# A Fourier mixing layer with its two products taken in the other order, beside attention in one kernel

## The chip, the cores and the metric

The kernel runs on one core of one Trainium2 chip. The metric is device time in microseconds of one execution. All inputs and outputs are float32 in the chip's memory (DRAM). The engines are TensorE (PE; its weight load is PEld), VectorE (DVE), ScalarE (ACT), GpSimd (POOL) and SyncE (SP), which issues every transfer of this kernel.

## The reference

Two layers on separate inputs of 2048 rows and 1024 channels, put side by side into one output of 2048 x 2048.

```python
def _A_ref(x, wqkv, wo):                 # attention, H = 32 heads of Dh = 32
    qkv = (x @ wqkv).reshape(B, S, 3, H, Dh).transpose(2, 0, 3, 1, 4)
    q, k, v = qkv[0], qkv[1], qkv[2]
    p = softmax(einsum("bhqd,bhkd->bhqk", q, k) * Dh ** -0.5)
    o = einsum("bhqk,bhkd->bhqd", p, v)
    return o.transpose(0, 2, 1, 3).reshape(B, S, D) @ wo

def _B_ref(x, dft_seq_re, dft_seq_im, dft_hid_re, dft_hid_im):   # Fourier mixing
    a = einsum("bsd,ed->bse", x, dft_hid_re)
    b = einsum("bsd,ed->bse", x, dft_hid_im)
    return einsum("ts,bse->bte", dft_seq_re, a) - einsum("ts,bse->bte", dft_seq_im, b)

return concatenate([_A_ref(...), _B_ref(...)], axis=-1)
```

With C for the cosine matrix over the sequence, N for the sine one, and R, I for the channel ones, the Fourier half is y = C (x R') - N (x I').

## The kernel before

**Dense products.** Every dense product (qkv, the two of the Fourier half, the output projection) is done in blocks of 128 x 512 with one step of Winograd's form of Strassen: a product of 2 x 2 halves takes 7 half-size products (numbered 1 to 7 in the code; `ORDER` is the order in which they are taken) and additions before and behind. Each operand tile is split into a rounded high part (a cast) and a residual (raw minus high), both in the fast float32 format, and each product of two tiles is three matmuls: high by high, low by high, high by low. So a block of depth 512 (4 chunks) is a **group** of 12 matmuls and one of depth 1024 a group of 24, all accumulating in one PSUM bank. `group` (L421) records them. `piece` makes a stationary operand of 4 chunks (tiles h and l), `moving` a moving one (a slot of two halves, twelve slots in a ring). Both call `fetch`, which loads one tile (raw), loads others (g) and adds or subtracts them on GpSimd or VectorE (L507), and `halves` (L528 cast, L531 residual).

**The Fourier half.** `dense1` takes x by both channel matrices: stationary x, 8 tiles, moving the 16 tiles of R and I; 7 x 8 x 2 groups of 12. It stores a = x R' and b = x I' as ab_d. `dense2` then does C a (m = 0) and N b (m = 1), 7 x 8 groups of 24 each; C and N are the stationary operands (in_ct), a and b the moving ones. The result of m = 0 goes to y_d, and behind m = 1 it is loaded again and the imaginary half subtracted from it (L1029). `gather` reads each finished group out of PSUM: it adds it to a running sum, kept in SBUF (slots 16 to 19, L984, L986) or in memory (class `Far`, x_d, L998, L1000), or to the sum that gives a result (L1024); what lies in memory is loaded into a tile c (L971), four of which go round.

**Attention.** Per head: scores of 128 x 1024 (L1322, two matmuls each), their row maxima on VectorE (L1328, negm), exponentials on ScalarE for the row sums (L1331); then transposed scores (L1447), exponentials of them (L1456) into tiles pt, and 64 small matmul records at a time with V (L1479).

**What sets the order.** All operations are recorded with their dependencies and given out by a planner (`Plan`, and the loop at the end) that keeps a clock per engine from fixed costs (a wide matmul 0.2274, a copy out of PSUM 0.685, a subtraction on GpSimd 1.31) and writes the order of every engine by hand. On TensorE the attention streams S, T and V alternate with the dense matmuls, which are called **fills** and come strictly in the order in which the dense functions record them: qkv, dense1, dense2, projection. A fill is given when its share of all fills is no further on than attention's share. Each engine then runs its own list in order and waits on semaphores where a producer is late.

Of the kernel before, what the change touches and what calls it, by code (L numbers as in the profile page):

```python
# [16 lines left out]
P = 128  # L17
# [208 lines left out]
def kernel(  # L226
# [25 lines left out]
    ab_d = [[[dram.tile([P, NB], F32, name=f"ab_d{m}_{e}_{k}") for k in range(NS)] for e in range(2)] for m in range(2)]  # L252
    s1_d = [dram.tile([P, 4, P], F32, name=f"s1_d{i}") for i in range(8)]
    t1_d = [dram.tile([P, NB], F32, name=f"t1_d{n}") for n in range(8)]
# [5 lines left out]
    u3_d = [[dram.tile([P, NB], F32, name=f"u3_d{i}_{m}") for m in range(2)] for i in range(8)]  # L260
    s2_d = [[dram.tile([P, 4, P], F32, name=f"s2_d{i}_{k}") for k in range(4)] for i in range(8)]
    t2_d = [[dram.tile([P, NB], F32, name=f"t2_d{m}_{k}") for k in range(8)] for m in range(2)]
    x_d = [[{w: dram.tile([P, NB], F32, name=f"x_d{i}_{m}_{w}") for w in (1, 6, 5)} for m in range(2)] for i in range(4)]
    u4_d = [[dram.tile([P, NB], F32, name=f"u4_d{m}_{i}") for i in range(8)] for m in range(2)]
    y_d = [[dram.tile([P, NB], F32, name=f"y_d{i}_{e}") for e in range(2)] for i in range(NS)]
# [119 lines left out]
    FILL = 3 * (7 * 24 * 4 + 7 * 16 * 4 + 7 * 8 * 16 + 2 * 8 * 4)  # L385
# [15 lines left out]
    banks = []  # L401
    fills = []
# [8 lines left out]
    def group(terms, n, finish):  # L411

        box = {}
        n *= 3
        k = 0
        for a, b in terms:
            for (u, v), after in (((0, 0), (a[0].made[0], b[0].made[0])), ((1, 0), (a[0].made[1],)), ((0, 1), (b[0].made[1],))):
                def emit(a=a, b=b, u=u, v=v, k=k):
                    if k == 0:
                        box["ps"] = bank()  # L420
                    nc.tensor.matmul(box["ps"], a[1]((a[0].hi, a[0].lo)[u]()), b[1]((b[0].hi, b[0].lo)[v]()), start=k == 0, stop=k == n - 1)  # L421

                o = op("PE", MM, emit, after, [a[0].users, b[0].users] if v else [])
                fills.append((o, k == 0, n - k))
                k += 1
        frees.append(finish(lambda: box["ps"], o))

    def groups(parts):
# [4 lines left out]
        for c in range(depth):  # L433
            for j, (u, v) in enumerate(((0, 0), (1, 0), (0, 1))):
                for i, (terms, _) in enumerate(parts):
# [10 lines left out]
                    fills.append((last[i], first, 3 * (depth - c) - j))  # L446
# [514 lines left out]
    def gather(what, X, Y, u3, to, wrote, part=None):  # L961
# [18 lines left out]
        def finish(ps, last):  # L980
# [25 lines left out]
            def put(at, ausers, alast, kind, to, wrote, part):  # L1006
# [15 lines left out]
                def emit():  # L1022
                    box["y"] = pre.tile([P, NB], F32, name="e", tag="e", bufs=NE)
                    nc.vector.tensor_tensor(out=box["y"], in0=at(), in1=ps(), op=kind)  # L1024
# [6 lines left out]
                wrote.append(op("SP", ISSUE, lambda: nc.sync.dma_start(to, box["y"]), [done], [users], rank, 256))  # L1031
# [27 lines left out]
    ab_st = [[[[] for _ in range(NS)] for _ in range(2)] for _ in range(2)]  # L1059

    def dense1():
        s1 = [[] for _ in range(8)]
        s2 = [[] for _ in range(8)]
        t1 = [[] for _ in range(8)]
        u3 = [[[], []] for _ in range(8)]

        def a_terms(p, i):
            q = lambda r, k: xb[8 * r + i, :, 4 * k : 4 * k + 4, :]
            return {
                1: [(1, q(0, 0), [])], 2: [(1, q(0, 1), [])], 4: [(1, q(1, 1), [])],  # L1070
                5: [(1, q(1, 0), []), (1, q(1, 1), [])],
                6: [(1, q(1, 0), []), (1, q(1, 1), []), (-1, q(0, 0), [])],
                7: [(1, q(0, 0), []), (-1, q(1, 0), [])],
                3: [(1, q(0, 1), []), (-1, s1_d[i], s1[i])],
            }[p]

        def b_terms(p, n):
            m, c = divmod(n, 4)
            q = lambda k, e: wd[m, 4 * k + c, :, e * NB : e * NB + NB]
            return {  # L1080
                1: [(1, q(0, 0), [])], 2: [(1, q(1, 0), [])], 3: [(1, q(1, 1), [])],
                5: [(1, q(0, 1), []), (-1, q(0, 0), [])],
                6: [(1, q(1, 1), []), (-1, q(0, 1), []), (1, q(0, 0), [])],
                7: [(1, q(1, 1), []), (-1, q(0, 1), [])],
                4: [(1, t1_d[n], t1[n]), (-1, q(1, 0), [])],
            }[p]

        def load_b(x, n):
            p = ORDER[x]
            B[x][n] = moving((8 * x + n) % 12, b_terms(p, n), (t1_d[n], t1[n]) if p == 6 else None)  # L1090

        B = [[None] * 8 for _ in ORDER]
        for n in range(4):
            load_b(0, n)
        X = {}
        for x, p in enumerate(ORDER):
            for i in range(8):
                a = piece(a_terms(p, i), (s1_d[i], s1[i]) if p == 6 else None)
                if i == 0:
                    for n in range(4, 8):  # L1100
                        load_b(x, n)
                if p == 1:
                    X[i] = accs(SUMS[i]) if i < 4 else [Far(x_d[i - 4][m]) for m in range(2)]
                for m in range(2):
                    h = DONE.get(p)
                    to = ab_d[m][h[1]][8 * h[0] + i] if h else None
                    group(
                        ((chunk(a, c), (B[x][4 * m + c], whole)) for c in range(4)), 4,
                        gather(p, X[i][m], None, (u3_d[i][m], u3[i][m]), to, ab_st[m][h[1]][8 * h[0] + i] if h else None),
                    )  # L1110
                if i % 2:
                    load_b(x + 1, i // 2) if x < 6 else load_ab(0, i // 2)

    AB = {}
    t2 = [[[] for _ in range(8)] for _ in range(2)]

    def load_ab(step, k):
        m, x = divmod(step, 7)
        p = ORDER[x]

        q = lambda r, e: (ab_d[m][1 - e][8 * r + k], ab_st[m][1 - e][8 * r + k])
        terms = {
# [4 lines left out]
            4: [(1, t2_d[m][k], t2[m][k]), (-1, *q(1, 0))],  # L1127
        }[p]
        AB[step, k] = moving((8 * (7 + step) + k) % 12, terms, (t2_d[m][k], t2[m][k]) if p == 6 else None)

    def dense2():

        y_st = [[[], []] for _ in range(NS)]
        u4 = [[[] for _ in range(8)] for _ in range(2)]
        for m in range(2):
            s2 = [[[], []] for _ in range(8)]

            def a_terms(p, i, k0):
                q = lambda r, k: ct[8 * r + i, :, 16 * m + 8 * k + k0 : 16 * m + 8 * k + k0 + 4, :]
                return {  # L1140
                    1: [(1, q(0, 0), [])], 2: [(1, q(0, 1), [])], 4: [(1, q(1, 1), [])],
                    5: [(1, q(1, 0), []), (1, q(1, 1), [])],
                    6: [(1, q(1, 0), []), (1, q(1, 1), []), (-1, q(0, 0), [])],
                    7: [(1, q(0, 0), []), (-1, q(1, 0), [])],
                    3: [(1, q(0, 1), []), (-1, s2_d[i][2 * m + k0 // 4], s2[i][k0 // 4])],
                }[p]

            X = {}
            for x, p in enumerate(ORDER):
                step = 7 * m + x  # L1150
                for i in range(8):
                    if p == 1 and i % 2 == 0:
                        X[i // 2] = accs(SUMS[i // 2])

                    def terms():
                        for k in range(0, 8, 4):
                            if i == 0 and k:
                                for c in range(4, 8):
                                    load_ab(step, c)
                            a = piece(a_terms(p, i, k), (s2_d[i][2 * m + k // 4], s2[i][k // 4]) if p == 6 else None)  # L1160
                            for c in range(4):
                                yield chunk(a, c), (AB[step, k + c], whole)

                    h = DONE.get(p)
                    t, e = (8 * h[0] + i, 1 - h[1]) if h else (0, 0)
                    to = out[t * P : t * P + P, D + e * NB : D + e * NB + NB] if m else y_d[t][e]
                    group(
                        terms(), 8,
                        gather(p, X[i // 2][i % 2], None, (u4_d[m][i], u4[m][i]), to,
                               [] if m else y_st[t][e], (y_d[t][e], y_st[t][e]) if m and h else None),  # L1170
                    )
                    if step < 13 and i % 2:
                        load_ab(step + 1, i // 2)
# [376 lines left out]
    done = 0.0  # L1550
# [5 lines left out]
    while nf < len(fills) or any(place[n] < len(s) for n, s in streams.items()):  # L1556
# [56 lines left out]
        if nf < len(fills):  # L1613
            o, first, left = fills[nf]
# [7 lines left out]
        if fill is not None and (not ok or (not first and left <= HB) or nf / (FILL - RES) <= done / ATT):  # L1622
            pl.start(fill)
            nf += 1
# [55 lines left out]
```

## Time and profile before

| | |
|---|---|
| runs | 2941.31, 2941.32, 2941.8 us; median 2941.32 |
| profiled execution, its span | 2940.6 us |
| granted TensorE clock | 1.000 |
| TensorE busy | 2931.5 us, 14922 matmul records |
| VectorE, ScalarE, GpSimd busy | 2275.1, 2271.7, 956.6 us |
| dense1: first store of a running sum (x_d), last store of a result (ab_d) | 842.6, 1472.8 us |
| dense2: first and last load of a second operand from ab_d, last load of y_d | 1305.0, 2700.3, 2777.2 us |
| end of the last attention matmul, of the last matmul | 2747.8, 2936.8 us |

A row of the groups gives line, engine, operation, output and inputs, count, then busy time, the mean of one in ns, and the idle time ahead of them with what ended it. A row of the windows gives a stretch, its length, and per engine the busy time and count (PE, PEld, DVE, ACT, POOL), the granted clock, the share of the transfer engines and GB/s. A row of the chain or the timeline gives a start and a length in us. "128x512" is partitions by elements.

### The profile page before, as it was taken

How to read it: one execution, taken by the hardware profiler on the slowest of the kernel's cores; microseconds unless marked ns; L12 is line 12 of the kernel's file. 1: busy time of each engine (PE TensorE's matmuls, PEld its weight loads, DVE VectorE, ACT ScalarE, POOL GpSimd, SP SyncE). 2: the span in 40 equal slices, each digit the busy share in tenths (PEclk: the TensorE clock that was granted, in tenths of full speed). 3: DMA queues.
4: the chain of work that ended last, by engine and by line, in shares of the span. 5: the costliest groups of instructions: out<-in, count | busy, mean ns of one | idle time of the engine just before them, and what ended most of it. 6: DMA issues, size and time to landing. Idle time of an engine off the chain costs nothing.

```text
span 2940.6 us, 45778 instructions
## 1 busy us (share of the span) xinstructions
PE 2931.5 (100%) x14922; PEld 2151.9 (73%) x14922; DVE 2275.1 (77%) x3103; ACT 2271.7 (77%) x4322; POOL 956.6 (33%) x746
## 2 busy tenths in 40 slices
PE   9999999999999999999999999999999999999999
PEld 7887777677777777777777777777777777677787
DVE  6778888788877877877677888787787788886685
ACT  5348888888888888888888888888888888886331
POOL 2323435222204432231112454433112454454142
PEclk9999999999999999999999999999999999999999
DMA  9975658666637655675434776655434786665753
GB/s 348 356 249 183 200 183 276 227 213 225 218 103 229 217 176 164 212 226 166 158 101 147 239 231 205 189 180 169 129 113 132 216 270 200 194 182 191 264 194 126
DMA packets 393880, 587.96 MB, mean 200 GB/s; under 512 B 112782, under 2 KB 114574, under 8 KB 393518
## 3 DMA queue, kind: packets, MB, share of 16 engines
q1 hardware_dynamic: 393644, 585.05, 61.8%
q8 instruction: 120, 1.97, 0.3%
q14 instruction: 116, 0.95, 0.1%
HBM read 421.30 MB, written 163.59 MB: 199 GB/s over the span
## 4 chain that ended last, share of the span: by engine, by line
PE 98%; DVE 1%; DMA 1%; ACT 0%; SPq 0%; issue 0%; DVEq 0%; ACTq 0%
PE pd L421 44%; PE psT L1447 16%; PE psS L1322 16%; PE pd L1479 15%; PE psT L421 6%; DVE negm L1328 0%; DMA er<-in_xa 0%; DVE l L531 0%; DMA qs<-qk_d 0%; PE psT L443 0%; ACT psS L1331 0%; DVE h L528 0%; PE pd L443 0%; ACT slot L527 0%; DVE slot L531 0%
## 5 line engine op out<-in xcount | busy, mean ns | idle before, releaser
L1328 DVE TENSOR_REDUCE negm<-psS 128x1 f32<-128x1024 f32 x1024 | 1242.8, 1221 | 226.4 <-PE psS L1322 215.2
L1331 ACT ACTIVATE psS<-psS,negm 128x1024 f32<-128x1024 f32 x1024 | 1223.9, 1195 | 71.8 <-DVE negm L1328 70.0
L421 PE MATMUL pd<-slot,h 128*128 128x512 f32 x3360 | 1144.0, 390 | 0.0
L1456 ACT ACTIVATE pt<-psT 128x512 f32<-128x512 f32 x1296 | 782.6, 697 | 260.1 <-PE psT L1447 237.2
L1447 PE MATMUL psT<-qs,ks 128*128 128x512 f32 x2048 | 794.3, 394 | 1.3 <-DMA qs<-qk_d 1.3
L421 PEld LDWEIGHTS pd<-slot,h 128*128 128x128 f32 x3360 | 630.7, 188 | 132.0
L421 PE MATMUL pd<-slot,l 128*128 128x512 f32 x1680 | 654.6, 390 | 0.0
L507 POOL TENSOR_TENSOR raw<-raw,g 128x512 f32<-128x512 f32 x295 | 382.6, 1304 | 483.8 <-DVE l L531 63.8
L1447 PEld LDWEIGHTS psT<-qs,ks 128*128 128x128 f32 x2048 | 381.8, 188 | 137.3 <-issue 45.3
L1322 PE MATMUL psS<-ks,qs 128*128 128x512 f32 x1552 | 473.4, 390 | 1.2 <-ACT psS L1331 1.2
L531 POOL TENSOR_TENSOR l<-raw,h 128x512 fp32r<-128x512 f32 x157 | 202.5, 1290 | 554.6 <-PE psT L1447 236.6
L531 POOL TENSOR_TENSOR slot<-raw,slot 128x512 fp32r<-128x512 f32 x156 | 201.0, 1293 | 518.0 <-DVE slot L528 146.3
L421 PEld LDWEIGHTS pd<-slot,l 128*128 128x128 f32 x1680 | 315.3, 188 | 67.0 <-issue 0.8
L1479 PE MATMUL pd<-pt,vt 128*32 128x512 f32 x2592 | 345.8, 594 | 0.0
L1322 PEld LDWEIGHTS psS<-ks,qs 128*128 128x128 f32 x1552 | 290.8, 188 | 64.0 <-ACT psS L1331 3.8
L1331 ACT ACTIVATION_READ_ACCUMULATOR psS<-psS,negm 128x1 f32 x1024 | 321.6, 314 | 0.0
L1456 ACT ACTIVATE ptm<-psT 128x512 f32<-128x512 f32 x392 | 242.6, 715 | 49.7 <-PE psT L1447 46.7
L1456 ACT ACTIVATE ptl<-psT 128x512 f32<-128x512 f32 x360 | 223.5, 708 | 31.0 <-PE psT L1447 30.2
L1479 PEld LDWEIGHTS pd<-pt,vt 128*32 128x32 f32 x2592 | 89.4, 110 | 180.3 <-issue 168.2
L421 PE MATMUL pd<-slot,slot 128*128 128x512 f32 x768 | 193.0, 391 | 0.0
L421 PEld LDWEIGHTS pd<-slot,slot 128*128 128x128 f32 x768 | 144.1, 188 | 31.2
L528 DVE CAST h<-raw 128x512 fp32r<-128x512 f32 x321 | 149.1, 467 | 14.5 <-PE pd L421 12.3
(139 smaller groups left out, 2323.8 us busy)
## 6 DMA issues: line engine op xcount, KB each, us to landing
raw<-in_ct SPq DMA_DIRECT2D x224, 256.0 KB
g<-in_ct SPq DMA_DIRECT2D x128, 256.0 KB
c<-u_d SPq DMA_DIRECT2D x120, 256.0 KB
qk_d<-e SPq DMA_DIRECT2D x52, 512.0 KB
qs<-qk_d SPq DMA_DIRECT2D x128, 192.0 KB
ks<-qk_d SPq DMA_DIRECT2D x128, 192.0 KB
raw<-ab_d SPq DMA_DIRECT2D x96, 256.0 KB
g<-ab_d SPq DMA_DIRECT2D x80, 256.0 KB
```

The source lines that it names most:

```text
L421: nc.tensor.matmul(box["ps"], a[1]((a[0].hi, a[0].lo)[u]()), b[1]((b[0].hi, b[0].lo)[v]()), start=k == 0, stop=k == n - 1)
L507: return (nc.gpsimd if e == "POOL" else nc.vector).tensor_tensor(out=dest(), in0=dest() if a is None else a.get(), in1=other["q"] if "q" i ...
L528: return nc.vector.tensor_copy(hi(), raw())
L531: return (nc.gpsimd if e == "POOL" else nc.vector).tensor_tensor(out=lo(), in0=raw(), in1=f(hi()), op=ALU.subtract)
L1322: nc.tensor.matmul(p[:, i * NB : i * NB + NB], (QX[0] if own else QS[h % 2])[:, qt * P : qt * P + P], KS[h % 2][:, c * 1024 + i * NB : c * ...
L1328: nc.vector.tensor_reduce(out=ST["negm"][:, c, qt : qt + 1], in_=box["p"], axis=AX.X, op=ALU.max, negate=True)
L1331: nc.scalar.activation(box["p"], box["p"], AF.Exp, bias=ST["negm"][:, c, qt : qt + 1], accum_out=ST["sums"][:, c, qt : qt + 1])
L1447: nc.tensor.matmul(box["p"], KS[h % 2][:, t * P : t * P + P], QS[h % 2][:, j * NB : j * NB + NB], start=True, stop=True)
L1456: nc.scalar.activation(box["t"], box["p"], AF.Exp)
L1479: nc.tensor.matmul(po["p"][j * DH : j * DH + DH, :], VT[h][:, k, :], box["t"], start=(k == t0), stop=(k == t), tile_position=(0, j * DH),)
```

## The change

The Fourier half is rearranged as y = [x' C' | -(x' N')]' [R' ; I']. `dense1` now sums over the sequence: x (by channel, stationary) times C' and N' together, 1024 x 2048 by 2048 x 4096 as seven half-size products in the order 1, 5, 2, 6, 7, 4, 3 (`OUTER`), each of 4 x 4 groups of 24. The results ut_d have channels on the partitions, and the N part is negated as it leaves PSUM. `dense2` takes ut_d as the stationary operand, 2048 deep (1024 channels of each part), against R and I stacked: 7 x 8 groups of 24, whose results go straight to the output. y_d and its addition are gone.

In `dense1` a stationary operand is made once per product and held over its four moving steps (`held`), half of them in the slots 16 to 19 that held sums. The running sums X and Y of all 16 blocks live in memory (xx_d, yy_d): every group's read-out but those of product 1 loads one or two of them (c, now L1179) and stores one or two, and products 6 and 7 read the PSUM bank twice. ut_d is stored so that four 128-wide blocks can be loaded each as one stationary tile; its stores have runs of 128 elements (512 B).

The inputs xb and ct are laid out differently in memory to fit. The new file also has code for a second level of splitting (`split`, `inner`, `HEAVY`, weights of the fills); the tuple `SPLIT` that chooses products for it is empty, so all weights are 1 and it is never called. Nothing else is changed; lines move (L421 to L417, L528 to L524, L531 to L527, L1322 and L1328 to L1534 and L1540, L1447 to L1659, L1479 to L1691).

```diff
-    FILL = 3 * (7 * 24 * 4 + 7 * 16 * 4 + 7 * 8 * 16 + 2 * 8 * 4)
+    SPLIT = ()
+    HEAVY = 1.5
+    FILL = 3 * (7 * 24 * 4 + 7 * 16 * 8 - 16 * len(SPLIT) + 7 * 8 * 8 + 2 * 8 * 4)
...
+    def merge(dst, acc, ps, kind, neg):
+        if not neg:
+            nc.vector.tensor_tensor(out=dst, in0=acc, in1=ps, op=kind)
+        elif kind == ALU.add:
+            nc.vector.scalar_tensor_tensor(out=dst, in0=ps, scalar=-1.0, in1=acc, op0=ALU.mult, op1=ALU.subtract)
+        else:
+            nc.vector.tensor_tensor(out=dst, in0=ps, in1=acc, op=ALU.subtract)
...
+    OUTER = (1, 5, 2, 6, 7, 4, 3)
+    DONE_IN = {2: (0, 0), 7: (1, 1), 3: (0, 1), 4: (1, 0)}
+    def outer(p, X, Y, to, wrote, neg):
...
+        x = stored(X.first if p == 2 else X.kept) if p in (2, 4, 5, 6, 7) else None
+        y = stored(Y.kept) if p in (3, 6, 7) else None
...
+            if p == 5:
+                return result(x, ALU.add, False, Y.to[5], Y)
+            if p == 6:
+                result(x, ALU.add, False, X.to[6], X)
+                return result(y, ALU.add, False, Y.to[6], Y)
+            if p == 7:
+                result(y, ALU.add, neg, to, None)
+                return result(x, ALU.add, False, X.to[7], X)
+            return result(y if p == 3 else x, ALU.subtract if p == 4 else ALU.add, neg, to, None)
...
     def dense1():
...
+        def simple(p):
...
+            for n in range(4):
+                M = []
+                def load(m, k):
+                    if n == 0:
+                        A[m, k] = held(fetch([P, 4, P], a(m, k), keep_a(m, k)), None if m < 2 else 12 + 2 * m + k)
+                for k in range(2):
+                    load(0, k)
+                    for c in range(4 * k, 4 * k + 4):
+                        M.append(moving((8 * z + c) % 12, b(n, c), keep_b(n, c)))
...
+                for m in range(4):
+                    group(((chunk(A[m, k], c), (M[4 * k + c], whole)) for k in range(2) for c in range(4)), 8,
+                          outer(p, X[m][n], Y[m][n], *out_to, h is not None and h[1] == 1))
...
     def dense2():
...
+            AB[step, k] = moving((8 * step + k) % 12, moving_terms(p, lambda r, e: (wd[r, k, :, e * NB : e * NB + NB], []), (t2_d[k], t2[k])),
...
+            q = lambda r, k: (ut_d[k][2 * r + i // 4][k0 // 4][i % 4], ut_st[k][2 * r + i // 4][k0 // 4])
...
-        "xb": c(B_x[0].reshape(NS, P, NC, P).transpose(0, 3, 2, 1)),
+        "xb": c(B_x[0].reshape(NS, P, NC, P).transpose(2, 1, 0, 3)),
-        "ct": c(np.stack([cr, ci]).reshape(2, NS, P, NS, P).transpose(1, 4, 0, 3, 2).reshape(NS, P, 2 * NS, P)),
+        "ct": c(np.stack([cr.T, ci.T]).reshape(2, NS, P, S)),
```

How the instructions move is read from the order in which each engine has them. First **TensorE at the first matmul of dense1**, before and then now; slot_7702 and slot_7790 are the first moving tiles, h and l the two parts of the stationary one.

```order
L421 MATMUL pd<-slot_7702,h 128x512
L1447 MATMUL psT<-qs_529,ks_530 128x512
L421 MATMUL pd<-slot_7702,l 128x512
L421 MATMUL pd<-slot_7702,h 128x512
L421 MATMUL pd<-slot_7745,h 128x512
L421 MATMUL pd<-slot_7745,l 128x512
L1322 MATMUL psS<-ks_530,qx 128x512 x2
```

```order
L417 MATMUL pd<-slot_7790,h 128x512
L1659 MATMUL psT<-qs_329,ks_330 128x512
L417 MATMUL pd<-slot_7790,l 128x512
L417 MATMUL pd<-slot_7790,h 128x512
L417 MATMUL pd<-slot_8054,h 128x512
L417 MATMUL pd<-slot_8054,l 128x512
L1534 MATMUL psS<-ks_330,qx 128x512 x2
```

The dense matmuls lie among the attention ones in the same way; the group now goes on over eight moving tiles in place of four. Over the whole list the counts of matmuls by shape are equal. Behind the last V matmul 833 dense matmuls stood, and 822 stand now.

Second, **VectorE in the later part of dense1**: negm is the row maximum of a score tile, e a result or a sum on its way to memory, c a loaded partial sum, pd a PSUM bank. Before, in the last product of dense1:

```order
L1024 TENSOR_TENSOR e<-slot_9251,pd 128x512
L528 CAST h<-raw 128x512
L1328 TENSOR_REDUCE negm<-psS 128x1 x2
L1024 TENSOR_TENSOR e<-c,pd 128x512
L1328 TENSOR_REDUCE negm<-psS 128x1 x3
```

Now, in a product whose read-outs are double:

```order
L527 TENSOR_TENSOR slot_15306<-raw,slot_15306 128x512
L1540 TENSOR_REDUCE negm<-psS 128x1 x3
L960 TENSOR_TENSOR e<-c,pd 128x512 x2
L1540 TENSOR_REDUCE negm<-psS 128x1 x4
L1567 TENSOR_REDUCE lh<-negm 128x16
```

Two read-outs, each with a loaded tile, stand together where one stood.

Third, **SP, which issues the transfers**, in the last product of dense1 before, and in product 7 now:

```order
L1031 DMA ab_d_0_12_245<-e 128x512
L971 DMA c<-u_d_1_394 128x512
L491 DMA raw<-in_ct 128x512
L1423 DMA vt<-v_d_127 128x4x32
L1031 DMA ab_d_0_13_214<-e 128x512
L971 DMA c<-u_d_0_395 128x512
L315 DMA ks_2490<-qk_d_0_98 96x512
```

```order
L968 DMA ut_d_0_1_310<-e 128x4x128
L968 DMA xx_d_0_7_406<-e 128x512
L1179 DMA c<-xx_d_0_6_437 128x512
L1179 DMA c<-yy_d_0_6_501 128x512
L496 DMA g<-in_ct 128x512 x3
L487 DMA raw<-in_ct 128x512 x5
L1635 DMA vt<-v_d_127 128x4x32
```

A group of product 7 stores a block of the result and a sum and loads two sums. Over the whole list SP has 2552 transfers in place of 2544.

357 lines of the change are left out of this document (245 added, 112 removed).

## The prediction

> **What bounds the kernel now.** I read the page first: busy times, slices, the chain of waits.
>
> ```profile
> span 2940.6 us, 45778 instructions
> PE 2931.5 (100%) x14922; PEld 2151.9 (73%) x14922; DVE 2275.1 (77%) x3103; ACT 2271.7 (77%) x4322; POOL 956.6 (33%) x746
> ...
> DMA  9975658666637655675434776655434786665753
> GB/s 348 356 249 183 200 183 276 227 213 225 218 103 229 217 176 164 212 226 166 158 101 147 239 231 205 189 180 169 129 113 132 216 270 200 194 182 191 264 194 126
> ...
> PE 98%; DVE 1%; DMA 1%; ACT 0%; SPq 0%; issue 0%; DVEq 0%; ACTq 0%
> ```
>
> TensorE is busy throughout, and the chain that ends last lies on it for 98%. Busy is not yet full pace, so I take the pace from the chain in order of time, at the end, where only wide matmuls run, and from one batch of attention-times-V matmuls.
>
> ```profile
> 2740.80 7.00 PE pd L1479 x64
> ...
> 2847.08 5.44 PE psT L421 x24
> ```
>
> A wide matmul costs 5.44/24 = 0.2267 us, a V record 7.00/64 = 0.1094 us. Then I count both kinds over 840 to 2740 us, which lies inside the Fourier part: first all of TensorE, then the lines L421 (dense work), L1322 and L1447 (scores), L1479 (V).
>
> ```profile
> 840.00:2740.00 1900.00, 1898.76 (x9915) 1369.87 (x9914) 1470.27 (x1984) 1604.53 (x3081) 638.98 (x496) 1.00 0.59 184
> ...
> 840.00:2740.00 1900.00, 1107.84 (x3765) 706.40 (x3764) 1.00 0.59 184
> ...
> 840.00:2740.00 1900.00, 453.57 (x1492) 279.26 (x1492) 1.00 0.59 184
> ...
> 840.00:2740.00 1900.00, 605.85 (x1562) 291.17 (x1562) 1.00 0.59 184
> ...
> 840.00:2740.00 1900.00, 342.32 (x3096) 95.59 (x3096) 1.00 0.59 184
> ```
>
> Wide: 3765 + 1492 + 1562 = 6819, by 0.2267 is 1545.9 us. V: 3096 by 0.1094 is 338.7. Together 1884.6 of 1900: 15.4 us are left that are not full pace. Part of that belongs to the 3096/64 = 48.4 V batches themselves, as the timeline around one shows.
>
> ```profile
> 1499.37 0.61 PE L1322 MATMUL psS<-ks,qx 128*128 128x512 f32 x2
> 1499.91 0.62 PE L1479 MATMUL pd<-pt,vt 128*32 128x512 f32 x2
> ...
> 1506.92 0.73 PE L1447 MATMUL psT<-qs,ks 128*128 128x512 f32 x2
> 1507.49 1.08 PE L1322 MATMUL psS<-ks,qx 128*128 128x512 f32 x4
> ```
>
> Two matmuls before the batch take 0.54 and two behind it 0.57, where 0.453 is full pace: 0.20 us a batch, 48.4 x 0.20 = 9.7 us. So 15.4 - 9.7 = 5.7 us is all that stalls and rounding can hold in these 1900 us. **TensorE's own pace bounds this kernel, stage by stage.** Where it does wait is named in its waits:
>
> ```profile
> PE pd L1555 <- DVE qs L303: 1.5, 1, 1.5
> PE psT L443 <- DVE acc L799: 1.3, 1, 1.3
> PE psT L1447 <- DMA qs<-qk_d: 1.3, 1, 1.3
> PE psS L1322 <- ACT psS L1331: 1.2, 3, 0.5
> ```
>
> The first two are the program's start, which the change leaves alone. The fourth is the kind that matters below.
>
> **The change, part by part: TensorE.** Both versions use one Winograd step in each of two products. Before, 7 x 16 x 4 x 3 = 1344 matmuls for x times the channel matrices and 7 x 16 x 8 x 3 = 2688 for the sequence; now 2688 for the sequence first and 7 x 8 x 8 x 3 = 1344 for the channels. 4032 either way, all 128x512. The order has as many matmuls of each shape as before, so this term is 4032 x 0.2267 = 914.1 us less 914.1 us = 0. No V batch is added either. Behind the last V matmul 822 dense matmuls follow instead of 833; those 11 (2.5 us) have moved in among the attention, not gone.
>
> **Evacuations and partial sums.** Groups of 24 matmuls replace half of the groups of 12: 224 groups become 168. The order's counts give VectorE 48 fewer PSUM reads in sum (copy, add, subtract), GpSimd or VectorE 40 fewer two-operand preparations and 32 fewer additions of the imaginary half to the real one; residuals (raw minus its rounded half) change engine, 9 from VectorE to GpSimd. Their prices:
>
> ```profile
> L1328 DVE TENSOR_REDUCE negm<-psS 128x1 f32<-128x1024 f32 x1024 | 1242.8, 1221 | 226.4 <-PE psS L1322 215.2
> ...
> L531 DVE TENSOR_TENSOR l<-raw,h 128x512 fp32r<-128x512 f32 x164 | 120.7, 740 | 3.1
> ...
> L1024 DVE TENSOR_TENSOR e<-c,pd 128x512 f32<-128x512 f32 x85 | 57.8, 680 | 11.4 <-PE pd L421 10.3
> L507 DVE TENSOR_TENSOR raw<-raw,g 128x512 f32<-128x512 f32 x77 | 55.5, 728 | 3.3 <-POOL raw L507 1.8 <-DMA g<-in_ct 1.3 <-issue 0.2
> ...
> L1029 DVE TENSOR_TENSOR e<-c,e 128x512 f32<-128x512 f32 x15 | 11.9, 796 | 0.1
> ...
> L507 POOL TENSOR_TENSOR raw<-raw,g 128x512 f32<-128x512 f32 x295 | 382.6, 1304 | 483.8 <-DVE l L531 63.8 <-issue 48.2 <-DMA raw<-in_xb 44.9
> L531 POOL TENSOR_TENSOR l<-raw,h 128x512 fp32r<-128x512 f32 x157 | 202.5, 1290 | 554.6 <-PE psT L1447 236.6 <-PE pd L421 127.7 <-DVE h L528 111.4
> ...
> L1029 POOL TENSOR_TENSOR e<-c,e 128x512 f32<-128x512 f32 x17 | 22.0, 1294 | 37.2 <-DVE h L528 26.5 <-DVE e L1024 9.7 <-DMA g<-ab_d 1.0
> ```
>
> VectorE: 48 x 0.680 + 13 x 0.728 + 15 x 0.796 + 9 x 0.740 = 60.7 us less. GpSimd: 27 x 1.304 + 17 x 1.294 - 9 x 1.290 = 45.6 us less. None of it lies on the path: it runs beside TensorE, which sets the end. It can only give back stalls, so its value is between 0 and the 5.7 us above; I take 0, because a stall comes from where a burst of VectorE work stands, not from its sum. Thirty-two of the subtractions become a fused one (PSUM times -1, then minus); its nearest row among the PSUM reads is 0.680, and even at the 0.796 of the addition from SBUF the 32 would add 3.7 us to an engine with 23% idle.
>
> **Partial sums now live in memory.** In the first product 128 evacuations of the 144 need a tile loaded first (two each in two of the seven products). All told, loads of partial sums go from 192 to 200, operand seconds from 280 to 240, stores of prepared operands from 64 to 104: 8 transfers of 256 KB more, 2 MB of 588 MB. The densest product is the fourth, with 16 loads of moving operands, 8 stores of them, 8 loads and 8 stores of sums in a step of 96 matmuls. At 1900/3765 = 0.505 us per dense matmul that is 40 x 0.262 MB in 48.4 us, 217 GB/s; with the lowest slice of now, 101 GB/s, for attention, 318, and the first two slices moved 348 and 356. So it is hidden, with little room in that product. If it weren't, 40 transfers at 348 less 101 GB/s take 42.5 us, still within the step.
>
> The 64 stores of the transposed result go out in runs of 512 B, 512 packets where 128 were.
>
> ```profile
> DMA packets 393880, 587.96 MB, mean 200 GB/s; under 512 B 112782, under 2 KB 114574, under 8 KB 393518
> ...
> q1 hardware_dynamic: 393644, 585.05, 61.8%
> ```
>
> A packet took 0.618 x 16 x 2940.6 / 393644 = 0.074 us on average. 64 x 384 more packets are at most 24576 x 0.074 / 16 = 114 us of the engines (if a quarter packet cost the average), and at least 0; the four products that store last 4 x 384 x 0.505 = 776 us, and at the 0.59 share of the row above 41% of that, 318 us, is idle to hold them. I take 0. The Trainium skill ("DMA: Bandwidth & Descriptors", Specifications) puts the line-rate minimum at 512 B, with read-modify-write below; by it these stores sit just on the good side, and the time stays the same; no row here has that size apart.
>
> **What a stall costs.** VectorE takes its work in order. These are the chain of waits at the largest stall of the Fourier part, and two rows of TensorE's timeline there:
>
> ```profile
> 2476.66 1.01 DVE h L528
> ...
> 2477.69 1.66 DVE l L531
> 2479.35 1.15 DVE negm L1328
> ...
> 2480.58 1.21 ACT psS L1331 x2
> ...
> 2480.98 0.39 PE L421 MATMUL pd<-slot,l 128*128 128x512 f32 x1
> ...
> 2481.84 0.73 PE L1322 MATMUL psS<-ks,qs 128*128 128x512 f32 x2 [0.47 <-ACT psS L1331]
> ```
>
> Two casts and two subtractions, 2.67 us, stood ahead of a row maximum; the exponential started late, and the next score matmul waited. Start to start TensorE took 0.86 us where 0.227 is full pace, so the burst cost 0.63 us. In the new order the pairs of evacuations (the fourth and fifth product read each PSUM bank twice) are 2 x 0.680 = 1.36 us, half such a burst, and stand between maxima. I expect no more stalls than now: term 0, with bounds of -5.7 (all gone) and +32 x 0.63/2 = 10 (each of the 32 pairs costs half of that burst).
>
> **The sum.** Span 2940.6 + 0 (matmuls) + 0 (evacuations) + 0 (transfers) + 0 (stalls) = 2940.6. The runs' median is 2941.3, 0.7 above the span. Forecast **2941.3 us**, no change. Within 0.2% is +-5.9 us, about what this kernel's measurement can tell.
>
> **Rivals.** *Slower: bursts on VectorE.* The mechanism of those rows at the 32 double evacuations, each of which also waits for two loads. If each costs the full 0.63 us, and the stall also holds up what VectorE has queued behind it (casts for the next group, the next row maximum), I get 20 us: 2961. It decides from 5.9/0.63 = 10 such stalls on. For it: loads now stand ahead of nearly every evacuation of the first product. Against it: the trace's 85 evacuations of a loaded tile waited for TensorE in 10.3 of their 11.4 us, not for a load, and VectorE has 60.7 us less to do. Chance 0.14; 10 to 16 stalls (2947 to 2951) are the likelier part of it.
>
> *Faster: fewer handovers.* There are 56 groups less, and VectorE is freer. All stalls gone is 5.7 us: 2935.6, just short of what can be told. Chance of more than 5.9 us 0.04.
>
> *The handover between the products.* The second product can't start a tile before the first has stored it. Its first product reads the parts that products 2 and 4, third and sixth of seven, finished; the last one's parts are read 192 matmuls in, 192 x 0.505 = 97 us later. If that failed, TensorE would still have attention to run; I price it at the longest landing in the chain once the matmuls run (first row below, from the chain in order of time), 5.6 us: 2947. Chance 0.02, counted with slower.
>
> ```profile
> 395.18 5.64 DMA qs<-qk_d
> ...
> L1555 PE MATMUL pd<-qs 96*128 96x512 f32 x10 | 4.6, 644 | 1.5 <-DVE qs L303 1.5
> ```
>
> *A cold array.* The ten first matmuls (second row, from the groups by line) took 644 ns each, so a long wait could cost twice. Behind 2747.8 us, where no attention is left to fill in, one wait of 5.6 us with ten matmuls behind it at 4.6/10 = 0.46 instead of 0.227 is 5.6 + 2.3 = 7.9 us: 2949. The longest wait on TensorE here is 1.5 us. Chance 0.01, with slower. The Trainium skill ("TensorE: Matmul & The Clock Gate", the HAM clock gate) says that about 3.4 us without work halve the clock; the trace agrees as far as those ten go, though the granted clock of its rows reads 1.00 there too.
>
> *The change doesn't do what it says*: the second level of splitting in the new code is switched off by an empty tuple, so no matmul is saved; were it on, the count would fall. The order excludes it.
>
> **Chances.** Same 0.79, faster 0.04, slower 0.17 (0.14 + 0.02 + 0.01). Range 2936.5 to 2950: below, the forecast less most of the 5.7; above, most of the +10 bound, which takes in the handover and the cold array; outside lies the burst rival beyond 14 stalls. The no-change case alone is 2937 to 2946.
>
> **What would show it.** Right: TensorE x14922 at full pace, chain 98% on it, 840 to 2740 us again with some 15 us left over; VectorE near 2275 - 61 = 2214 us, GpSimd near 911; the end stretch at 5.44 us per 24. Wrong: score matmuls waiting for the exponential in tens of places in the first product; VectorE waiting for loads of sums; TensorE waiting at the handover.

## The result

The changed kernel takes 2968.89 us (median of 4 runs, 2967.49 to 2970.55) where the kernel before took 2941.32 beside it: a ratio of 1.0096, 95% interval 1.0082 to 1.0111. It is 27.6 us slower, and the forecast was no change. First the page of the changed kernel.

```profile
span 2968.0 us, 45623 instructions
...
PE 2953.4 (100%) x14922; PEld 2152.6 (73%) x14922; DVE 2231.4 (75%) x3023; ACT 2276.2 (77%) x4319; POOL 909.0 (31%) x709
...
q1 hardware_dynamic: 419372, 587.15, 61.9%
...
PE 97%; DMA 1%; DVE 1%; ACT 0%; SPq 0%; issue 0%; DVEq 0%; ACTq 0%
...
L417 PE MATMUL pd<-slot,h 128*128 128x512 f32 x2464 | 842.7, 390 | 0.0
...
L417 PE MATMUL pd<-slot,slot 128*128 128x512 f32 x2112 | 600.1, 394 | 0.0
```

TensorE does the same 14922 records, is again busy throughout, and the chain is on it for 97%. Busy time says nothing here. The last two rows hint at something: matmuls whose two operands both lie in slots take 394 ns from start to modelled end, those whose stationary operand is a piece h take 390.

**Where the time is.** The prediction's count over 840 to 2740 us, made again (one row each for L417, the dense work, L1534 and L1659, the scores, and L1691, V):

```profile
840.00:2740.00 1900.00, 1096.36 (x3707) 695.80 (x3707) 1.00 0.59 183
...
840.00:2740.00 1900.00, 457.07 (x1492) 279.33 (x1492) 1.00 0.59 183
...
840.00:2740.00 1900.00, 597.29 (x1532) 285.45 (x1532) 1.00 0.59 183
...
840.00:2740.00 1900.00, 342.32 (x3096) 95.59 (x3096) 1.00 0.59 183
```

6731 wide matmuls by 0.2267 are 1525.9 us, 3096 V records by 0.1094 are 338.7, together 1864.6: 35.4 us are left that are not full pace, where 15.4 were left before. That is 20.0 us of the loss, at a granted clock that reads 1.00. The waits of TensorE can't fill it:

```profile
PE psS L1534 <- ACT psS L1543: 3.8, 6, 1.2
PE psT L417 <- ACT slot L523: 3.1, 2, 2.1
...
PE psT L417 <- DVE slot L527: 0.7, 1, 0.7
```

Of these only the first lies in that stretch, and it is 3.8 us. The rest has to be pace, and TensorE's timeline shows it, at the change from one group of the sequence product to the next.

```profile
1055.26 0.61 PE L1534 MATMUL psS<-ks,qs 128*128 128x512 f32 x2
...
1057.30 0.61 PE L1534 MATMUL psS<-ks,qs 128*128 128x512 f32 x2
...
1057.98 0.40 PE L417 MATMUL pd<-slot,slot 128*128 128x512 f32 x1
1058.22 0.40 PE L1659 MATMUL psT<-qs,ks 128*128 128x512 f32 x1
1058.45 1.09 PE L417 MATMUL pd<-slot,slot 128*128 128x512 f32 x4
1059.38 0.62 PE L1534 MATMUL psS<-ks,qs 128*128 128x512 f32 x2
1059.85 0.39 PE L1659 MATMUL psT<-qs,ks 128*128 128x512 f32 x1
```

From 1055.26 to 1057.30 nine matmuls start (two, and seven in the rows left out), one every 0.2267 us. From 1057.98, where the stationary operand comes from a slot instead of h, to 1059.85 eight start, one every 0.2338, with no wait marked. The attention matmuls between them are at the slower pace too. So half of the groups of dense1, those with their held operand in slots 16 to 19 (m = 2 and 3 in `held`), run 3% slower.

**The other loss is at the end**, at the start of the output projection:

```profile
2803.76 0.84 PE L417 MATMUL psT<-slot,slot 128*128 128x512 f32 x3
2805.57 0.49 PE L417 MATMUL psT<-slot,slot 128*128 128x512 f32 x1 [0.97 <-ACT slot L523]
2806.77 0.73 PE L417 MATMUL psT<-slot,slot 128*128 128x512 f32 x2 [0.70 <-DVE slot L527]
2809.59 3.58 PE L417 MATMUL psT<-slot,slot 128*128 128x512 f32 x6 [2.09 <-ACT slot L523]
2812.96 7.12 PE L417 MATMUL pd<-slot,slot 128*128 128x512 f32 x24
2819.92 2.43 PE L417 MATMUL psT<-slot,slot 128*128 128x512 f32 x10
```

The first twelve matmuls take 9.20 us where 12 x 0.2267 = 2.72 is full pace, the next 24 take 6.96 instead of 5.44: 8.0 us. Up to 2809.59 six matmuls take 5.83 us instead of 1.36, so 4.5 us go with the waits (3.8 as marked). The thirty behind it take 10.33 us instead of 6.80, so 3.5 us are lost there, most of them to the clock, as the windows of TensorE show (records that lie in the window in part or whole, then the granted clock). Seven matmuls stand in 3.19 us there, the last of them 0.63 long, so one starts every 0.427 us:

```profile
2812.96 3.19 PE L417 MATMUL pd<-slot,slot 128*128 128x512 f32 x7
```

```profile
2812.90:2816.00 3.10, 3.10 (x9) 0.50 1.03 386
2816.50:2819.90 3.40, 3.40 (x16) 1.00 1.04 378
```

ScalarE's timeline and the chain of waits say what was late:

```profile
2799.20 2.67 ACT L523 ACTIVATE slot<-raw 128x512 fp32r<-128x512 f32 x4 [2.54 <-PE psT L417]
```

```profile
2804.00 4.89 DMA raw<-o_d
...
2808.91 0.64 ACT slot L523
```

Four casts wait for TensorE before they may write their slots. By my reading they hold raw tiles meanwhile, of which this stage has five (`Ring(5)`), and the load of the attention's output that the third wait needs starts at 2804.00. The slots are the point: the ring of the channel product, `(8 * step + k) % 12`, ends in slots 0 to 7, and the output projection puts its first moving tiles in slots 0 to 3. Before, the ring ran on from dense1, ended in slots 4 to 11 and left 0 to 3 free.

The same collision, smaller, stands between the two products of the Fourier half: step 0 of the channel product wants the slots that dense1's last groups hold.

```profile
2173.07 0.41 PE L417 MATMUL pd<-slot,h 128*128 128x512 f32 x1
2173.82 0.73 PE L1534 MATMUL psS<-ks,qs 128*128 128x512 f32 x2 [0.34 <-ACT psS L1543]
...
2175.89 0.74 PE L1534 MATMUL psS<-ks,qs 128*128 128x512 f32 x2 [0.59 <-ACT psS L1543]
...
2177.40 0.39 PE L1659 MATMUL psT<-qs,ks 128*128 128x512 f32 x1
```

For 4.33 us TensorE has hardly anything but attention, and attention alone goes at the pace of the exponentials: nine matmuls start where 19 could, 2.3 us lost.

### The profile page after: what moved, and what is told of

The parts are those of the page before. It is cut to its first block, busy times and chain, and to the rows that moved or that the text cites. A ratio compares the mean times of both kernels' runs of the same rounds, so it can differ in the third digit from the quotient of the medians.

```text
span 2968.0 us, 45623 instructions
## 1 busy us (share of the span) xinstructions
PE 2953.4 (100%) x14922; PEld 2152.6 (73%) x14922; DVE 2231.4 (75%) x3023; ACT 2276.2 (77%) x4319; POOL 909.0 (31%) x709
## 3 DMA queue, kind: packets, MB, share of 16 engines
q1 hardware_dynamic: 419372, 587.15, 61.9%
## 4 chain that ended last, share of the span: by engine, by line
PE 97%; DMA 1%; DVE 1%; ACT 0%; SPq 0%; issue 0%; DVEq 0%; ACTq 0%
PE pd L417 44%; PE psT L1659 16%; PE psS L1534 16%; PE pd L1691 15%; PE psT L417 6%; DVE negm L1540 0%; DMA raw<-o_d 0%; PE psT L439 0%; DMA m_d<-lt 0%; DMA er<-in_wv 0%; DMA t<-in_wo 0%; DMA a<-o_d 0%; DMA er<-in_xa 0%; DVE h L524 0%; ACT psS L1543 0%; DMA s<-o_d 0%
## 5 line engine op out<-in xcount | busy, mean ns | idle before, releaser
L1540 DVE TENSOR_REDUCE negm<-psS 128x1 f32<-128x1024 f32 x1024 | 1243.2, 1221 | 285.9 <-PE psS L1534 275.7
L417 PE MATMUL pd<-slot,h 128*128 128x512 f32 x2464 | 842.7, 390 | 0.0
L1659 PE MATMUL psT<-qs,ks 128*128 128x512 f32 x2048 | 797.8, 395 | 0.1
L527 POOL TENSOR_TENSOR slot<-raw,slot 128x512 fp32r<-128x512 f32 x245 | 315.7, 1294 | 975.0 <-DVE slot L524 510.7
L417 PE MATMUL pd<-slot,slot 128*128 128x512 f32 x2112 | 600.1, 394 | 0.0
L417 PEld LDWEIGHTS pd<-slot,h 128*128 128x128 f32 x2464 | 462.6, 188 | 97.7 <-issue 0.8
L1659 PEld LDWEIGHTS psT<-qs,ks 128*128 128x128 f32 x2048 | 381.8, 188 | 143.6 <-issue 48.6
L417 PE MATMUL pd<-slot,l 128*128 128x512 f32 x1232 | 480.3, 390 | 0.2 <-DVE l L527 0.2
L1534 PE MATMUL psS<-ks,qs 128*128 128x512 f32 x1552 | 476.4, 392 | 3.8 <-ACT psS L1543 3.8
L503 POOL TENSOR_TENSOR raw<-raw,g 128x512 f32<-128x512 f32 x268 | 346.8, 1302 | 395.9 <-DMA raw<-in_ct 71.2
L417 PEld LDWEIGHTS pd<-slot,slot 128*128 128x128 f32 x2112 | 397.8, 188 | 91.4
L1691 PE MATMUL pd<-pt,vt 128*32 128x512 f32 x2592 | 345.8, 594 | 0.0
L1534 PEld LDWEIGHTS psS<-ks,qs 128*128 128x128 f32 x1552 | 290.6, 188 | 70.6 <-ACT psS L1543 7.8
L417 PEld LDWEIGHTS pd<-slot,l 128*128 128x128 f32 x1232 | 231.3, 188 | 48.9 <-DVE l L527 0.5
L1691 PEld LDWEIGHTS pd<-pt,vt 128*32 128x32 f32 x2592 | 89.4, 110 | 180.6 <-issue 170.0
L527 POOL TENSOR_TENSOR l<-raw,h 128x512 fp32r<-128x512 f32 x79 | 101.9, 1290 | 249.3 <-PE psT L1659 103.9
L524 DVE CAST slot<-raw 128x512 fp32r<-128x512 f32 x369 | 167.5, 474 | 8.3 <-POOL raw L503 6.4
```

The source lines that it names most:

```text
L503: return (nc.gpsimd if e == "POOL" else nc.vector).tensor_tensor(out=dest(), in0=dest() if a is None else a.get(), in1=other["q"] if "q" i ...
L524: return nc.vector.tensor_copy(hi(), raw())
L527: return (nc.gpsimd if e == "POOL" else nc.vector).tensor_tensor(out=lo(), in0=raw(), in1=f(hi()), op=ALU.subtract)
L1534: nc.tensor.matmul(p[:, i * NB : i * NB + NB], (QX[0] if own else QS[h % 2])[:, qt * P : qt * P + P], KS[h % 2][:, c * 1024 + i * NB : c * ...
L1540: nc.vector.tensor_reduce(out=ST["negm"][:, c, qt : qt + 1], in_=box["p"], axis=AX.X, op=ALU.max, negate=True)
L1659: nc.tensor.matmul(box["p"], KS[h % 2][:, t * P : t * P + P], QS[h % 2][:, j * NB : j * NB + NB], start=True, stop=True)
```

## The experiments

Two theories were to be tested: that the **place** of the operands sets the pace of a matmul, and that the two **collisions of slots** make the rest. The compiler's memory map gives the places. On the right side of the on-chip memory (slots 0 to 11, h and l, q and k) every tile starts at 480 beyond a multiple of 512 bytes; on the left side (loads, slots 12 to 19, V) at 384. A small tile ahead of a side shifts all that comes behind it. It adds no instruction, and the order of every engine stays as it is.

**The left side moved by 32 bytes**, in the changed kernel and in the one before:

```diff
-    const = ctx.enter_context(tc.tile_pool(name="const", bufs=1))
+    const = ctx.enter_context(tc.tile_pool(name="const", bufs=1)); pad = const.tile([P, 8], F32, name="pad")
```

> The changed kernel with one 32-byte tile added ahead of everything on the left side of the on-chip memory; no instruction is added or reordered, but every left-side tile (loads, slots 12 to 19, softmax and attention tiles) moves up by 32 bytes, to the same remainder mod 64 bytes as the right-side tiles (slots 0 to 11, pieces, q and k). Alignment theory: a matmul is slower when one of its two operands starts at a multiple of 64 bytes (left side) while the other does not; so the matmuls of the sequence product whose held piece lies in slots 16 to 19 come back from about 0.234 us to 0.227 us: 1000 to 1100 us holds about 507 matmul records instead of 503, 1600 to 1700 about 525 instead of 498, and the whole goes from 2968.9 to about 2953 us, a few us lower still (2949) if the V part of the projections at 200 to 790 us is slow for the same reason. Rival, region: slots 16 to 19 lie low in the memory, far from the rest, and 32 bytes change nothing: 2968.9 us, 503 and 498 records. Rival, what the held pieces need (traffic on ScalarE, VectorE or the transfers beside them): 2968.9 us as well.

> The kernel before with the 32-byte tile added on the left side: no instruction is added or reordered, all operands of its matmuls come to the same remainder mod 64 bytes. Alignment theory: its only slow matmuls are those of the V part and its neighbours between 200 and 790 us (some 0.23 us instead of 0.227), so it gains about 3 us: 2938 us. Region or traffic: 2941.3 us.

Measured: 2961.36 us (ratio to the kernel before 1.0066, 1.0051 to 1.0081), 7.5 us less than the changed kernel and half of what the theory asked; the kernel before with the same tile 2940.50, ratio 0.9997 (0.9987 to 1.0006), no change that can be told. An edit that only moves tiles is worth 7.5 us, so neither traffic nor the region, which both expected no change, can be the sole reason. But the remainder mod 64, as I had put it, is not the whole of it: the two sides agree in it now, yet not mod 128.

**The right side moved.**

```diff
-    big = ctx.enter_context(tc.tile_pool(name="big", bufs=1, side="right"))
+    big = ctx.enter_context(tc.tile_pool(name="big", bufs=1, side="right")); pad = big.tile([P, 8], F32, name="pad")
```

> The changed kernel with the same 32-byte tile added ahead of everything on the right side instead: all right-side tiles move down by 32 bytes to multiples of 64 bytes, where the left-side tiles lie already. No instruction is added or reordered. If a mixture of two alignments in one matmul is what is slow: everything pairs alike, about 2953 us, as with the left side moved. If an operand on a multiple of 64 bytes is slow in itself: now all wide matmuls run at about 0.234 us, 12,000 of them by 0.006 us, some 70 us more: about 3030 us. If the region or the traffic is the reason: 2968.9 us, unchanged.

Measured: 2999.02 us, ratio 1.0195 (1.0180 to 1.0211), 30.1 us more than the changed kernel and none of the three values expected. My description of the edit was wrong: the tile came to lie behind slots 0 to 11, which stayed at 480, while h, l, q, k and the slots from 20 on went to 448. That makes it a better test, since now nearly every dense matmul mixes the two, and both kinds stand side by side in TensorE's timeline:

```profile
110.62 2.96 PE L417 MATMUL psT<-slot,slot 128*128 128x512 f32 x12
113.42 5.69 PE L417 MATMUL pd<-slot,slot 128*128 128x512 f32 x24
118.94 5.60 PE L417 MATMUL psT<-slot,slot 128*128 128x512 f32 x24
124.38 2.88 PE L417 MATMUL pd<-slot,slot 128*128 128x512 f32 x12
127.10 0.40 PE L417 MATMUL pd<-slot,h 128*128 128x512 f32 x1
```

The first twelve have one operand in slots 8 to 11 (480) and the other in 36 to 39 (448): 2.80 us, 0.2333 each. The next 24 take 5.52 us, 0.230 on the mean. The 24 from 118.94 have both in slots 32 to 39 (448): 5.44 us, 0.2267 each. So no remainder is slow in itself, and it takes no low place in the memory either: the pace drops where the two operands of the matmuls start at different remainders.

**All at one remainder.** The left side moved by 96 bytes, to 480 like the right one (the line as above with `[P, 24]`); beside it 64 bytes (`[P, 16]`), which leaves 448 against 480.

> The changed kernel with a left-side tile of 96 bytes instead of 32. Slots 0 to 11, the pieces, q and k all start at remainder 480 of 512 bytes; the left-side tiles start at 384 in the changed kernel, at 416 with 32 bytes (where the matmuls of the held pieces in slots 16 to 19 took 231 ns instead of 233) and now at 480 like the others. No instruction is added or reordered. Theory, two operands at different offsets within a line of memory slow a matmul: now the sequence product's matmuls take 227 ns throughout, the mean of the stretch from 800 to 2170 us falls from about 230.2 ns to 227.1, and the time is 2968.9 - 15.6 = 2953 us, less 2 to 3 us in the V part of the projections: 2950 us. Rival, half of it is the region (slots 12 to 19 lie low): the pace stays at about 231 ns for those groups, and the time near the 2961.4 us that 32 bytes gave. Rival, the remainder mod 64 alone counts and the rest of the loss is another one: 2961.4 us too.

> The changed kernel with a left-side tile of 64 bytes: the left-side tiles start at remainder 448 of 512 bytes, the others at 480, the remainders mod 64 are as in the changed kernel. Theory of different offsets mod 64: as the changed kernel, 2968.9 us. If only the distance to the other operand mod 128 or more counts: a value between 2953 and 2969 us. If any shift of the left side helps: 2961 us or less.

Measured: 2950.94 us (ratio 1.0033, 1.0020 to 1.0045) with 96 bytes, 18.0 us less than the changed kernel; 2964.36 (1.0080, 1.0066 to 1.0094) with 64. The theory of offsets had said 2950 for the first; the second lies between the two kernels, not at the 2968.9 that the remainder mod 64 alone would give. With 96 bytes the timeline shows the groups held in slots at full pace, ten matmuls in 2.26 us between these two rows,

```profile
1056.97 0.62 PE L1534 MATMUL psS<-ks,qs 128*128 128x512 f32 x2
...
1059.23 0.62 PE L1534 MATMUL psS<-ks,qs 128*128 128x512 f32 x2
```

and the page's groups by line give both-in-slots matmuls the 390 ns of the others:

```profile
L417 PE MATMUL pd<-slot,slot 128*128 128x512 f32 x2112 | 590.6, 390 | 0.0
```

Offsets of 96, 64 and 32 bytes between the sides give 2968.89, 2961.36 and 2964.36 us, none 2950.94. The cost is not in proportion to the offset. Whether 128 bytes apart would count as equal wasn't tried.

**The slots of the ring.**

```diff
-            AB[step, k] = moving((8 * step + k) % 12, moving_terms(
+            AB[step, k] = moving((8 * step + k + 8) % 12, moving_terms(
...
-            1: ([20, 24], 0), 7: ([4, 8], 20), 2: ([0, 4], 24), 6: ([8, 0], 20),
-            5: ([4, 8], 24), 3: ([0, 4], 20), 4: ([8, 0], 24),
+            1: ([20, 24], 4), 7: ([8, 0], 20), 2: ([4, 8], 24), 6: ([0, 4], 20),
+            5: ([8, 0], 24), 3: ([4, 8], 20), 4: ([0, 4], 24),
```

> The changed kernel with the ring of the channel product's moving tiles begun four slots on (step 0 in slots 8 to 11 and 0 to 3, the last step again in 8 to 11 and 0 to 3) and the output projection's slots below 12 turned by four, so that its first moving tiles take slots 4 to 7, which the last step of the channel product does not use. Slot theory: the tail's loss (waits of 3.8 us at the start of the output projection and matmuls at 0.427 us behind them, some 8 us in all) and the 1.9 us at the handover between the two products go: 2800 to 2900 us of the span holds about 443 matmul records instead of 408, and the time is 2958 to 2960 us. Rival: the wait is one for the attention's outputs, stored last at about 2770 us, and the slots only happen to be busy: 2967 to 2969 us.

Measured: 2957.49 us (ratio 1.0054, 1.0039 to 1.0069), 11.4 us less than the changed kernel. The window from 2800 us holds the 443 records that full pace gives:

```profile
2800.00:2900.00 100.00, 100.00 (x443) 1.00 0.57 191
```

The rival, that the attention's outputs come too late, falls: the last of them was stored from 2771.26 us on in the changed kernel, 32 us ahead of the projection's first matmul, and with other slots the wait is gone. At the handover the channel product's first group now runs through at full pace: between these rows 46 matmuls start in 10.45 us, where 10.43 is full pace.

```profile
2167.05 0.62 PE L1534 MATMUL psS<-ks,qs 128*128 128x512 f32 x2
...
2177.50 0.62 PE L1534 MATMUL psS<-ks,qs 128*128 128x512 f32 x2
```

By the rows the two collisions were worth 8.0 + 2.3 = 10.3 of the 11.4 us. **One collision alone**, by `(8 * step + k + 4) % 12` with the projection's slots left as they were, takes away the one at the end only:

> The changed kernel with only one of the two collisions of slots taken away: the channel product's ring begins four slots on (step 0 in slots 4 to 11, the last step in 4 to 11), so slots 0 to 3 are free when the output projection wants them, as in the kernel before; its first four tiles still fall on slots 4 to 7, which the last group of the sequence product holds. The operands' offsets stay as in the changed kernel. If the end was worth what the trace showed there (3.8 us of waits, matmuls at 0.427 us behind them, some 8 us in all) and the handover the rest of the 11.4 us that the full turn of the ring gave: 2960 to 2961 us, 443 matmul records between 2800 and 2900 us, and waits of about 1.9 us left at 2173 to 2177 us. If the end alone made all of the 11.4 us: 2957.5 us. If both have to be right for any of it: 2969 us.

Measured: 2963.56 us (1.0071, 1.0054 to 1.0087), 5.3 us less than the changed kernel and some 3 us above what I expected. The end is mended,

```profile
2800.00:2900.00 100.00, 100.00 (x443) 1.00 0.61 208
```

but the handover between the products got longer. Between these rows 17 matmuls start in 8.29 us where 3.85 is full pace, 4.4 us lost instead of 2.3:

```profile
2172.84 0.73 PE L1534 MATMUL psS<-ks,qs 128*128 128x512 f32 x2
...
2181.13 0.74 PE L1534 MATMUL psS<-ks,qs 128*128 128x512 f32 x2
```

So the end was worth its 8.0 us, and the handover took 2.1 of them back: -5.9 by the rows, -5.3 by the runs (-6.65 against the kernel before, which took 2942.64 beside this run). Why the handover got longer is not shown; by the formulas the slots that the last group of dense1 releases last, 4 to 7, are now wanted by the first four tiles of the channel product instead of the second four. The ring has to be right at both ends.

**Both cures together, and the better layout in the kernel before.**

> The changed kernel with both: the channel product's ring begun four slots on with the output projection's slots turned to match (11.4 us on its own), and the left-side tile of 96 bytes. If the two causes are apart and both theories hold, the gains add: 2968.9 - 11.4 - 15.6 = 2942 us, less 2 to 3 us in the V part: about 2939 to 2940 us, 1 to 2 us below the kernel before. If the region is half of the pace: about 2950 us.

> The kernel before with the left-side tile of 96 bytes. Theory of offsets: the V part and its neighbours from 500 to 790 us (230.2 to 233.0 ns on the mean) come to 227, some 2.5 us: 2938 to 2939 us. Region or traffic: 2941 us, unchanged, as with 32 bytes (2940.5).

Measured: 2939.49 us for the changed kernel with both (ratio to the kernel before 0.9993, 0.9984 to 1.0002). The cures add: 2968.89 - 11.4 - 18.0 = 2939.5. The kernel before with 96 bytes takes 2937.16 us (0.9988, 0.9979 to 0.9997) and is the fastest of all that were run. It gains 4.0 us, in the V part of the projections, where tiles in slots 12 to 19 meet tiles on the right side. The unshifted kernel before had it in its trace: from one of these rows to the next nine matmuls start, in 2.11 us, 0.2344 each.

```profile
568.47 0.63 PE L1322 MATMUL psS<-ks,qs 128*128 128x512 f32 x2
...
570.58 0.63 PE L1322 MATMUL psS<-ks,qs 128*128 128x512 f32 x2
```

Of the 27.7 us (2968.89 less the 2941.19 of the larger number of runs) this settles:

| part | us | from |
|---|---|---|
| operands at different offsets in dense1 | 14.0 | 18.0 that 96 bytes give the changed kernel, less the 4.0 that they give the one before |
| the two collisions of slots | 11.4 | the turned ring |
| the change itself, on equal terms | 2.3 | 2939.49 - 2937.16, both with 96 bytes |

The runs of one kernel spread over 3 to 5 us, so by my estimate each part is good to 1 or 2 us. The last 2.3 us stands on 11 runs each (2937.56 to 2941.00 against 2936.07 to 2939.49) and lies inside the 5.9 us that the forecast counted as no change. In the trace with both cures TensorE waits 3.5 us for exponentials, in 5 places. One of them is the double evacuation that the prediction had named; VectorE's timeline there, and TensorE's:

```profile
1588.75 1.21 DVE L1540 TENSOR_REDUCE negm<-psS 128x1 f32<-128x1024 f32 x1
1589.88 0.68 DVE L962 SCALAR_TENSOR_TENSOR e<-pd,c 128x512 f32<-128x512 f32 x1
1590.48 0.67 DVE L960 TENSOR_TENSOR e<-c,pd 128x512 f32<-128x512 f32 x1
1591.08 1.21 DVE L1540 TENSOR_REDUCE negm<-psS 128x1 f32<-128x1024 f32 x1
```

```profile
1589.75 1.07 PE L417 MATMUL pd<-slot,slot 128*128 128x512 f32 x4
1591.31 0.73 PE L1534 MATMUL psS<-ks,qs 128*128 128x512 f32 x2 [0.49 <-ACT psS L1543]
```

Four matmuls and a wait take 1.56 us instead of 0.91: 0.65 us. The kernel before with 96 bytes waits 1.3 us for exponentials, in 4 places, so 2.2 us are new, as much as the 2.3. But the double evacuations don't explain most of it: ahead of the two longest waits, 0.95 us at 2477.78 and 1.38 at 2506.20, VectorE has casts and residuals (`l<-raw,h`) and no evacuation pair, and at about the same times the kernel before with 96 bytes waits too (0.31 and 0.51). What makes them longer is not shown, and no run took the double evacuations away.

## Why the prediction was wrong, point by point

- **TensorE, 4032 x 0.2267 less the same = 0: this step failed.** The count held (14922 records both times), the price didn't. It was one price for all wide matmuls, read at the end of the program, where both operands lie on the right side. The change puts half of the first product's stationary operands into slots 16 to 19, and a matmul of those starts every 0.2338 us in the rows above. The term was worth 14.0 us: 1344 such matmuls at 0.0071 more are 9.5, and the rest lies with the attention matmuls between them. It could have been seen: the rows at 568 us show that pace in the trace of before, but my check of the pace began at 840 us, behind the stage that has it.
- **Stalls, 0 with bounds of -5.7 and +10: too narrow a view.** It looked at VectorE's bursts among the attention. This step failed too: the 11.4 us came from reused slots, of which the sum had no term, though the two ring formulas stood in the diff.
- **A cold array, 2949, chance 0.01: it happened**, at the place given there, for another reason. That the size agrees (7.9 us; 8.0 measured) is partly luck: the prediction had one wait of 5.6 and 2.3 of slow matmuls; there were three waits, 4.5 us with them and 3.5 behind. The transfer was late because casts waited for slots, and no wait was longer than 2.09 us. I had taken the longest wait of before as evidence against it, and had not followed which slots would be free at that point. At the granted clock of 0.50 matmuls start every 0.427 us. "TensorE: Matmul & The Clock Gate" of the Trainium skill (Back-to-back issue gap) gives a 512-column matmul 512/1.2 = 427 ns on the cold clock; the trace agrees.
- **The handover between the products, 2947, chance 0.02:** real, but 2.3 us and for the slots, not for the stores of the first product.
- **VectorE's bursts, 2961, chance 0.14:** the price was right (0.65 us at one double evacuation, 0.63 predicted), the number was not: waits for exponentials rose from 3 places to 6, two of which stand at the handover, far from the 10 at which this rival decides.
- **Evacuations, hidden:** held. VectorE has 43.7 us less (60.7 predicted), GpSimd 47.6 less (45.6), and no time came of it.
- **Transfers, hidden:** held. The small stores and the other transfers add 25728 packets (24576 predicted from the stores alone), and the engines' share goes from 61.8% of 2940.6 us to 61.9% of 2968.0, some 20 us of the 0 to 114 that bounded it. TensorE waits for no transfer of the Fourier half.

The forecast for the change on equal terms, no change, came out at +2.3 us; what it left out was where the new code puts its tiles.

## What to carry to other kernels

A price per matmul belongs to a pair of places, not to a shape: when a change moves an operand to another pool, read the pace from a stretch of the trace that uses the same pair, start to start, and if it is above the best pace compare the tiles' byte offsets. When tiles rotate through fixed slots, write down for each handover which slots the last step holds and which the next step wants first. And a slowdown that leaves every engine as busy as before, with hardly a wait, is a change of pace; count matmuls by their full price over a long stretch and see what is left.

## What the runs showed that was not expected

Matmuls of 128 x 512 start every 0.2267 us when their two operands begin at the same remainder mod 512 bytes, and every 0.2333 to 0.2344 in the rows above when these differ by 32 or 96, at a granted clock of 1.00; 64 costs too, by the times. The attention matmuls among them slow down too, though their own operands agree; in a stretch of dense work alone the pace changes at once (118.94 us above). What in the memory makes it so is not shown, nor which two reads meet: weights are loaded beside running matmuls (PEld is busy 2152.6 us beside PE's 2953.4 in a span of 2968.0), so it may be one matmul's moving operand and the weights of the next, rather than the two operands of one; no run separates the two. "SBUF — State Buffer" of the Trainium skill (Who interferes with whom) gives TensorE two read ports, independent of each other, and says that it never waits for another engine. Here its pace hangs on how its own operands lie to each other, and the measurement decides: 96 bytes in front of the left side are worth 18.0 us, 0.6%.
